# A gated attention and maxout kernel on one core: the order of every engine fixed by hand, one copy per ff2, prefetches spread

## The chip, the cores and the metric

One core of one Trainium2 chip. The metric is the device time in microseconds (us). "Span" is the time from the first to the last instruction in a profile; the device time was 1.7 to 2.1 us longer. The profile names the engines PE (TensorE matmuls), PEld (TensorE weight loads), DVE (VectorE), ACT (ScalarE), POOL (GpSimd) and SP (SyncE).

## The reference

```python
# u, v: (8, 3072, 256)   z: (8, 3072, 64)   w1, w2: (256, 1024)   w_out: (1024, 256), all float32
def _attn_ref(u, v, z):
    scores = (1.0 / S) * np.matmul(z, z.transpose(0, 2, 1))
    attn = np.maximum(scores, 0.0) ** 2
    return u * np.matmul(attn, v)

def _moe_ref(x, w1, w2, w_out):
    return np.maximum(x @ w1, x @ w2) @ w_out

# reference: _moe_ref(_attn_ref(u, v, z).reshape(24576, 256), w1, w2, w_out)
```

The scores are symmetric. So the kernel computes only the blocks on and above the diagonal, and gets the mirrored ones by a transposing DMA. It also uses max(h1, h2) = relu(h1 - h2) + h2. So the first product is x (w1 - w2), called *ff1*; the second, *ff2*, is relu(ff1) w_out plus x (w2 w_out), with both weight differences and products folded once.

## The kernel before

The work comes in 48 groups: 8 batches of 6, each of 512 rows (four tiles of 128). A group has these matmuls:

- score pairs: two matmuls of 64 x 128 weights and 512 columns, one in each half of the array's rows; 42 pairs a batch in all
- attention: 24 units of two matmuls of 512 columns
- ff1 of the group before: 16 matmuls of 512 columns
- ff2 of the group before: 40 matmuls of 256 columns

In PSUM, where the matmuls write, the kernel keeps one accumulator of 2 x 512 fp32 columns and three buffers of the same size (tag `mm`). The three serve everything else in turn: a score pair (`s_ps`), two blocks of ff1 (`d_ps`), all of an ff2 (`o_ps`). To "evict" a buffer is to read it out, after which it is free again. The code, cut:

```python
def ff1(nb, xT, g_sb, on_dve):                  # four times a group, by DVE and ACT in turn
    d_ps = mm_psum.tile([P, 2, GW], fp32, name="d_ps", tag="mm")
    # ... four matmuls ...
    o = g_sb[:, nb : nb + 2, :]
    if on_dve:
        nc.vector.tensor_single_scalar(out=o, in_=d_ps, scalar=0.0, op=ALU.max)
    else:
        nc.scalar.activation(o, d_ps, AF.Relu)

def ff2(b, g, xT, g_sb):
    o_ps = mm_psum.tile([P, G, D], fp32, name="o_ps", tag="mm")
    o_sb = opool.tile([P, G, D], fp32, name="o_sb")
    for t in range(G):
        # ... eight matmuls g_sb x w_out, then two xT x W2o, into o_ps[:, t, :] ...
        if t % 2 == 1:
            nc.scalar.copy(o_sb[:, t - 1 : t + 1, :], o_ps[:, t - 1 : t + 1, :])
    nc.sync.dma_start(...)

with tc.manual_schedule(engines={PE}):          # only TensorE's order is as written
    # ... all scores of group 0 first ...
    for i, (b, g) in enumerate(groups):
        if g == 0 and b + 1 < B:                # all prefetches of a batch at its start
            zTs[b + 1] = zT_dma(load_z(b + 1, 1))
            v_of[b + 1] = load_v(b + 1, 2)
        if b + 1 < B:
            load_u(b + 1, g)
        # ... scores of the next group in up to four bursts, the four ff1 pieces between units:
        order = list(range(g * G, NT)) + list(range(0, g * G))     # mirrored blocks last
        for k, t in enumerate(order):
            for pr in at_w.get(k, ()):
                score_pair(*pr, zTs[nxt[0]])
            if k in at_f:
                ff1(at_f[k], prev[2], g_sb, on_dve=(at_f[k] // 2) % 2 == 0)
            attn_unit(b, g, t, v_of[b], xacc, k == 0, k == NT - 1)
        xT = epilogue(b, g, xacc)               # DVE: xT = xacc * u
        if prev:
            ff2(*prev, g_sb)
```

## Time and profile before

| | before |
|---|---|
| device time | 1108.57 us (1107.86 to 1109.05) |
| third group begins | 111.2 us |
| period of one batch of six groups, steady state | 128.86 us |
| of which matmuls of attention, ff1, ff2 back to back | 6 x 18.18 = 109.1 us |

(The first row is of three runs. With one more the median is 1108.21, which stands in the table of the result.) A batch's period is the distance in the timeline from the end of one ff2 to the end of the sixth after it. "Third group begins" is the first score matmul after the first ff2.

The page of the kernel before: parts 1 and 2, and groups of part 5 (line, engine, operation, tiles, shape, count; busy us and mean ns of one; idle us of the engine before them and who ended most of it).

```profile
span 1106.8 us, 13696 instructions
PE 1004.6 (91%) x5720; PEld 512.5 (46%) x5720; DVE 421.7 (38%) x556; ACT 472.2 (43%) x530; POOL 43.9 (4%) x86
...
PE   6318999999999999999999999999999999999997
...
PEclk8668999999999999999999999999999999999999
...
L203 PE MATMUL o_ps<-w_out_sb,g_sb 128*128 128x256 bf16 x1536 | 199.3, 272 | 32.6 <-ACT o_sb L219 32.3
L185 PE MATMUL d_ps<-xT,w_sb 128*128 128x512 bf16 x768 | 197.0, 380 | 0.0
...
L123 PE MATMUL s_ps<-zT 64*128 64x512 bf16 x672 | 107.9, 390 | 59.0 <-DVE W2o_sb L261 27.8
L219 ACT COPY o_sb<-o_ps 128x512 f32<-128x512 f32 x96 | 56.2, 585 | 245.5 <-PE o_ps L211 242.6
```

TensorE is the busy engine, and two things stand out. The second and third slices (28 to 83 us) are mostly empty, at a granted clock of about 0.6, and the fourth is not yet full, at about 0.8. And ff2 waits for its own copy.

Waits of VectorE (DVE) and TensorE (PE), some of the longest (us in total, times, longest us):

```profile
DVE zd L69 <- DMA zT<-zd: 55.6, 6, 31.8
...
PE o_ps L203 <- ACT o_sb L219: 32.3, 48, 0.7
...
DVE zd L69 <- DMA zn<-in_z_dram: 28.3, 3, 23.3
PE s_ps L123 <- DVE W2o_sb L261: 27.8, 1, 27.8
...
PE s_ps L123 <- ACT r_sb L134: 21.4, 6, 18.6
```

Behind TensorE's two long waits at the start (18.6 and 27.8 us) stand two z copies at the head of VectorE's queue. The first waited for its load, the second for the transpose that still read the same buffer:

```profile
44.96 1.03 DVE L69 COPY zd<-zn 128x1536 bf16<-128x1536 bf16 x2 [23.34 <-DMA zn<-in_z_dram]
83.73 1.03 DVE L69 COPY zd<-zn 128x1536 bf16<-128x1536 bf16 x2 [31.80 <-DMA zT<-zd]
```

Its TensorE timeline (start us, us, engine, line, operation, tiles, count; in brackets the idle time before and its releaser):

```profile
59.40 0.39 PE L123 MATMUL s_ps<-zT 64*128 64x512 bf16 x2
87.55 1.04 PE L123 MATMUL s_ps<-zT 64*128 64x512 bf16 x4 [27.76 <-DVE W2o_sb L261]
...
111.17 1.13 PE L123 MATMUL s_ps<-zT 64*128 64x512 bf16 x6
112.23 1.90 PE L166 MATMUL xacc<-a_sb,v_sb 128*128 128x512 bf16 x8
...
128.88 0.38 PE L211 MATMUL o_ps<-W2o_sb,xT 128*128 128x256 bf16 x2
129.94 1.03 PE L203 MATMUL o_ps<-w_out_sb,g_sb 128*128 128x256 bf16 x8 [0.67 <-ACT o_sb L219]
```

How to read the last two lines. Two matmuls start at 128.88, and 256 columns take 0.109 us each, so the next could start at 129.10. It starts at 129.94: 0.84 us are lost. The bracket says 0.67, because the profile counts idle time only from the modelled end of the matmul before, and a matmul's listed duration is longer than its spacing. In this document "lost" always means the distance from the natural start; it is the larger number.

### The profile page before, as it was taken

The page shows a single profiled execution, that of the slowest core. Times are in us where ns is not written, and L with a number is a line of the kernel's source. Part 1 is how long each engine was busy: PE and PEld are TensorE (multiplying, and loading weights), DVE is VectorE, ACT ScalarE, POOL GpSimd, SP SyncE. Part 2 cuts the span into 40 slices and gives each one's busy share as a digit, 9 for nine tenths or more (in the row PEclk, how much of TensorE's full clock was granted, in tenths as well). Part 3 has the DMA queues.
Part 4 walks back from the last instruction along what each step waited for, and adds up shares of the span by engine and source line. Part 5 has one row for each costly group of instructions (what it writes and reads, how often), then busy time and mean ns, then how long its engine had stood idle before and what let it go on. Part 6 is the DMA issues. An engine that isn't in the chain of part 4 may idle for free.

```text
span 1106.8 us, 13696 instructions
## 1 busy us (share of the span) xinstructions
PE 1004.6 (91%) x5720; PEld 512.5 (46%) x5720; DVE 421.7 (38%) x556; ACT 472.2 (43%) x530; POOL 43.9 (4%) x86
## 2 busy tenths in 40 slices
PE   6318999999999999999999999999999999999997
PEld 2103444445544554454454455445544545544554
DVE  5204334443354333533344332543334332443321
ACT  5213435543365434544255433653345442554322
POOL 3100000000000000000000000000000000000000
PEclk8668999999999999999999999999999999999999
DMA  9999856964699646995579754996559631653300
GB/s 167 134 189 174 144 99 129 167 144 96 100 175 173 110 94 119 147 189 105 94 137 162 145 96 96 124 207 122 92 102 203 122 86 48 115 115 76 77 39 38
DMA packets 341661, 136.94 MB, mean 124 GB/s; under 512 B 324064, under 2 KB 325344, under 8 KB 341600
## 3 DMA queue, kind: packets, MB, share of 16 engines
q1 hardware_dynamic: 328928, 106.19, 49.6%
q0 software_dynamic: 12672, 29.89, 20.2%
q8 instruction: 44, 0.72, 0.3%
q14 instruction: 17, 0.14, 0.0%
HBM read 59.77 MB, written 25.17 MB: 77 GB/s over the span
## 4 chain that ended last, share of the span: by engine, by line
PE 78%; ACT 8%; DMA 5%; issue 3%; DVE 3%; SPq 3%; POOL 0%; ACTq 0%; POOLq 0%; DVEq 0%
PE xacc L166 40%; PE o_ps L203 16%; PE d_ps L185 13%; PE s_ps L123 5%; PE o_ps L211 4%; ACT o_sb L219 4%; ACT r_sb L134 4%; DVE g_sb L194 2%; SPq L141 2%; DMA zn<-in_z_dram 1%; DMA uT<-un 1%; DMA un<-in_u_dram 1%; SPq L88 1%; DMA zT<-zd 1%; DVE a_sb L136 1%
## 5 line engine op out<-in xcount | busy, mean ns | idle before, releaser
L136 DVE TENSOR_TENSOR a_sb<-r_sb 128x1024 bf16<-128x1024 bf16 x336 | 231.1, 692 | 436.9 <-ACT r_sb L134 436.9
L134 ACT ACTIVATE r_sb<-s_ps 128x1024 bf16<-128x1024 f32 x332 | 318.4, 1027 | 164.1 <-PE s_ps L123 144.0
L166 PEld LDWEIGHTS <-v_sb 128*128 128x128 bf16 x2304 | 216.4, 98 | 288.1 <-issue 47.0
L166 PE MATMUL xacc<-a_sb,v_sb 128*128 128x512 bf16 x1344 | 326.9, 384 | 0.0
L166 PE MATMUL xacc<-at_sb,v_sb 128*128 128x512 bf16 x960 | 229.2, 379 | 0.0
L203 PE MATMUL o_ps<-w_out_sb,g_sb 128*128 128x256 bf16 x1536 | 199.3, 272 | 32.6 <-ACT o_sb L219 32.3
L185 PE MATMUL d_ps<-xT,w_sb 128*128 128x512 bf16 x768 | 197.0, 380 | 0.0
L196 ACT ACTIVATE g_sb<-d_ps 128x1024 bf16<-128x1024 f32 x96 | 98.4, 1025 | 214.2 <-PE d_ps L185 155.6
L203 PEld LDWEIGHTS <-g_sb 128*128 128x128 bf16 x1536 | 149.8, 98 | 68.8 <-issue 40.7
L123 PE MATMUL s_ps<-zT 64*128 64x512 bf16 x672 | 107.9, 390 | 59.0 <-DVE W2o_sb L261 27.8
L219 ACT COPY o_sb<-o_ps 128x512 f32<-128x512 f32 x96 | 56.2, 585 | 245.5 <-PE o_ps L211 242.6
L194 DVE TENSOR_SCALAR g_sb<-d_ps 128x1024 bf16<-128x1024 f32 x96 | 117.2, 1221 | 45.2 <-PE d_ps L185 33.4
L185 PEld LDWEIGHTS <-w_sb 128*128 128x128 bf16 x768 | 75.3, 98 | 90.9 <-issue 1.1
L171 DVE SCALAR_TENSOR_TENSOR xT<-xacc,uT 128x512 bf16<-128x512 f32 x96 | 61.8, 686 | 107.3 <-PE xacc L166 107.3
L123 PEld LDWEIGHTS <-zT 64*128 64x128 bf16 x672 | 28.5, 94 | 130.3 <-issue 121.3
L211 PE MATMUL o_ps<-W2o_sb,xT 128*128 128x256 bf16 x384 | 73.3, 273 | 0.0
L86 POOL DMA_DIRECT2D un<-in_u_dram x48 | 25.4, 530 | 651.2 <-DMA uT<-un 649.1
L69 DVE COPY zd<-zn 128x1536 bf16<-128x1536 bf16 (+1 forms) x18 | 8.6, 520 | 83.9 <-DMA zT<-zd 55.6
L211 PEld LDWEIGHTS <-xT 128*128 128x128 bf16 x384 | 37.6, 98 | 4.3
L78 POOL DMA_DIRECT2D v_sb<-in_v_dram x20 | 10.7, 545 | 110.1 <-PE xacc L166 110.1
L103 PE MATMUL tpz<-ident,zd 128*128 128x128 bf16 x24 | 3.1, 308 | 5.7 <-DVE zd L69 5.5
L67 POOL DMA_DIRECT2D zn<-in_z_dram x9 | 4.9, 547 | 42.6 <-DVE zd L69 41.8
(21 smaller groups left out, 24.2 us busy)
## 6 DMA issues: line engine op xcount, KB each, us to landing
out_dram<-o_sb SPq DMA_DIRECT2D x48, 512.0 KB, 4.9
un<-in_u_dram POOLq DMA_DIRECT2D x48, 256.0 KB, 4.9
v_sb<-in_v_dram POOLq DMA_DIRECT2D x14, 768.0 KB, 16.0
zn<-in_z_dram POOLq DMA_DIRECT2D x7, 384.0 KB, 4.6
at_sb<-a_sb SPq DMA_TRANSPOSE x120, 4.6
v_sb<-in_v_dram POOLq DMA_DIRECT2D x6, 256.0 KB, 7.9
uT<-un SPq DMA_TRANSPOSE x48, 3.1
w_121<-in_moe_w_dram POOLq DMA_DIRECT2D x1, 512.0 KB, 12.4
```

What stands on the lines that cost most here:

```text
L86: nc.gpsimd.dma_start(out=un, in_=src[:, ds(g * G, G), :])
L123: nc.tensor.matmul(s_ps[:, h, :], zT[rows, 2 * m + h, :], zT[rows, ds(g * G, G), :].rearrange("p t c -> p (t c)"), start=True, stop=True,)
L134: nc.scalar.activation(r, s_ps, AF.Relu)
L136: nc.vector.tensor_mul(a[:, k : k + 2, :], r, r)
L166: nc.tensor.matmul(o, v_sb[:, t, ts(dc, P)], mv, start=first, stop=last)
L171: nc.vector.scalar_tensor_tensor(out=xT[:, dc, :].rearrange("p (t r) -> p t r", r=P), in0=xacc[:, dc, :].rearrange("p (t r) -> p t r", r=P ...
L185: nc.tensor.matmul(d_ps[:, j, :], w15_sb[:, kc, ts(nb + j, P)], xT[:, kc, :], start=(kc == 0), stop=(kc == KD - 1),)
L194: nc.vector.tensor_single_scalar(out=o, in_=d_ps, scalar=0.0, op=ALU.max)
L196: nc.scalar.activation(o, d_ps, AF.Relu)
L203: nc.tensor.matmul(o_ps[:, t, :], g_sb[:, nb, ts(t, P)], w_out_sb[:, nb, :], start=(nb == 0), stop=False,)
L211: nc.tensor.matmul(o_ps[:, t, :], xT[:, dc, ts(t, P)], W2o_sb[:, dc, :], start=False, stop=(dc == KD - 1),)
L219: nc.scalar.copy(o_sb[:, t - 1 : t + 1, :], o_ps[:, t - 1 : t + 1, :])
```

## The change: its intent and the diff

The intent: let no engine's order be the scheduler's. Every queue is issued in the written order. Mirrored blocks come first in a group, because they were finished longest ago. Scores run ahead across group borders, in bursts of three pairs at units 0, 8 and 16. Each ff2 is copied out once. The next batch's z, u and v are loaded in portions over the groups. The diff, cut (the two lines with "takes all 1024 columns" sum up the code that was there; left out are the sizes of some buffer pools, the copy of W2o, which moved from VectorE to ScalarE, the first group's relus, a third of which VectorE did and which are all ScalarE's now, and the last ff2, written out in halves):

```diff
-    with tc.manual_schedule(engines={PE}):
+    with tc.manual_schedule():
...
 def ff1
-        if on_dve:  ... DVE takes all 1024 columns of this d_ps ...
-        else:       ... ACT takes all 1024 columns ...
+            nc.scalar.activation(g_sb[:, nb, :], d_ps[:, 0, :], AF.Relu)
+            nc.vector.tensor_single_scalar(
+                out=g_sb[:, nb + 1, :], in_=d_ps[:, 1, :], scalar=0.0, op=ALU.max
+            )
...
 def ff2
-            if t % 2 == 1:
-                nc.scalar.copy(o_sb[:, t - 1 : t + 1, :], o_ps[:, t - 1 : t + 1, :])
+            nc.scalar.copy(o_sb, o_ps)
...
+        double_z(0, 0, 4)
+        zT_pe(0, 0, 4, "dve")
+        double_z(0, 4, 8)
+        zT_pe(0, 4, 8, "act")
+        ahead(1)
+        double_z(0, 12, 8)
+        zT_pe(0, 12, 8, "dve")
+        ahead(2)
+        double_z(0, 20, 4)
+        zT_pe(0, 20, 4, "dve")
...
-            order = list(range(g * G, NT)) + list(range(0, g * G))
-            for k, t in enumerate(order):
+            for n in range(NT):
+                k = need[i, n]
+                if done < 12:
+                    ahead(max(k, done + 1))
+                elif k > done or (n in (0, 8, 16) and done + 3 <= k + AHEAD):
+                    ahead(done + 3)
+                attn_unit(b, g, n, acc, n == 0, n == NT - 1)
+                if n == 1 and i + 2 < len(groups):
+                    load_u(*groups[i + 2])
+                if i == 0 and n == 13:
+                    turn_u(0, 0)
+                if n == 20 and i + 1 < len(groups):
+                    turn_u(*groups[i + 1])
+                if b + 1 < B:
+                    if g == 1 and n == 4:
+                        load_z(b + 1, 0, NT)
+                    if g == 2 and n == 4:
+                        double_z(b + 1, 0, NT)
+                        zT_dma(b + 1)
+                    if g >= 1 and n == 8:
+                        load_v(b + 1, (g - 1) * G, G)
...
+            if prev:
+                g_sb = ff(prev)          # all four ff1 pieces, here
             xT = epilogue(b, g, acc)
             if prev:
                 ff2(*prev, g_sb)
```

One thing is easily missed in this diff: ff1 is no longer spread between attention units, but stands as one block directly before ff2. The built program shows another: VectorE's half of a `d_ps` waits for ScalarE's half, although the two read different halves of it.

More of the change, by code (lines that the diff above doesn't have):

```diff
@@ L27 @@
     ALU = mybir.AluOpType
-    PE = mybir.EngineType.PE
     B, S, D = u.shape
@@ L34 @@
     P = 128
+    R = 64
     NT = S // P
@@ L40 @@
     KF = Dff // P
+    AHEAD = 10
     c2 = float((1.0 / S) * (1.0 / S))
@@ L47 @@
     vpool = ctx.enter_context(tc.tile_pool(name="vpool", bufs=2))
-    unat = ctx.enter_context(tc.tile_pool(name="unat", bufs=4))
-    upool = ctx.enter_context(tc.tile_pool(name="upool", bufs=8))
-    apool = ctx.enter_context(tc.tile_pool(name="apool", bufs=8))
-    tpool = ctx.enter_context(tc.tile_pool(name="tpool", bufs=12))
-    rpool = ctx.enter_context(tc.tile_pool(name="rpool", bufs=4))
+    unat = ctx.enter_context(tc.tile_pool(name="unat", bufs=3))
+    upool = ctx.enter_context(tc.tile_pool(name="upool", bufs=4))
+    apool = ctx.enter_context(tc.tile_pool(name="apool", bufs=9))
+    tpool = ctx.enter_context(tc.tile_pool(name="tpool", bufs=13))
+    rpool = ctx.enter_context(tc.tile_pool(name="rpool", bufs=3))
     xpool = ctx.enter_context(tc.tile_pool(name="xpool", bufs=2))
@@ L57 @@
     acc_psum = ctx.enter_context(tc.tile_pool(name="acc_psum", bufs=1, space=bass.MemoryType.PSUM))
-    def load_z(b, chunks):
-        zn = znat.tile([P, NT, dqk], bf16, name="zn")
-        zd = znat.tile([P, NT, 2, dqk], bf16, name="zd")
-        src = z[b].rearrange("(p t) d -> p t d", t=NT)
-        n = NT // chunks
-        for c in range(chunks):
-            sl = ds(c * n, n)
-            nc.gpsimd.dma_start(out=zn[:, sl, :], in_=src[:, sl, :])
-            for h in range(2):
-                nc.vector.tensor_copy(zd[:, sl, h, :], zn[:, sl, :])
-        return zd
@@ L72, in load_v, with by_tile, load_z @@
-    def load_v(b, chunks):
-        v_sb = vpool.tile([P, NT, D], bf16, name="v_sb")
-        src = v[b].rearrange("(p t) d -> p t d", t=NT)
-        n = NT // chunks
-        for c in range(chunks):
-            sl = ds(c * n, n)
-            nc.gpsimd.dma_start(out=v_sb[:, sl, :], in_=src[:, sl, :])
-        return v_sb
-    uT = {}
+    def by_tile(x):
+        return x.rearrange("(p t) d -> p t d", t=NT)
+    zn, zd, zT, v_sb, un, uT = {}, {}, {}, {}, {}, {}
+    def load_z(b, lo, n):
+        if b not in zn:
+            zn[b] = znat.tile([P, NT, dqk], bf16, name="zn")
+            zd[b] = znat.tile([P, NT, 2, dqk], bf16, name="zd")
+            zT[b] = zpool.tile([P, NT, P], bf16, name="zT")
+        sl = ds(lo, n)
+        nc.gpsimd.dma_start(out=zn[b][:, sl, :], in_=by_tile(z[b])[:, sl, :])
@@ new lines, in double_z, with zT_dma, zT_pe @@
+    def double_z(b, lo, n):
+        sl = ds(lo, n)
+        for h in range(2):
+            nc.vector.tensor_copy(zd[b][:, sl, h, :], zn[b][:, sl, :])
+    def zT_dma(b):
+        nc.sync.dma_start_transpose(zT[b], zd[b].rearrange("p t h d -> p (t h d)"))
+    def zT_pe(b, lo, n, engine):
+        tp = mm_psum.tile([P, n, P], bf16, name="tpz", tag="mm")
+        for j in range(n):
+            nc.tensor.transpose(
+                tp[:, j, :], zd[b][:, lo + j, :, :].rearrange("p h d -> p (h d)"), ident
+            )
+        if engine == "act":
+            nc.scalar.copy(zT[b][:, lo : lo + n, :], tp)
+        else:
+            nc.vector.tensor_copy(zT[b][:, lo : lo + n, :], tp)
@@ L83, in load_u, with load_v @@
+    def load_v(b, lo, n):
+        if b not in v_sb:
+            v_sb[b] = vpool.tile([P, NT, D], bf16, name="v_sb")
+        sl = ds(lo, n)
+        nc.gpsimd.dma_start(out=v_sb[b][:, sl, :], in_=by_tile(v[b])[:, sl, :])
     def load_u(b, g):
-        un = unat.tile([P, G, D], bf16, name="un")
-        src = u[b].rearrange("(p t) d -> p t d", t=NT)
-        nc.gpsimd.dma_start(out=un, in_=src[:, ds(g * G, G), :])
+        un[b, g] = unat.tile([P, G, D], bf16, name="un")
+        nc.gpsimd.dma_start(out=un[b, g], in_=by_tile(u[b])[:, ds(g * G, G), :])
@@ L87, in load_u, with turn_u @@
+    def turn_u(b, g):
         t = upool.tile([P, G, KD, P], bf16, name="uT")
         nc.sync.dma_start_transpose(
-            t.rearrange("p a c r -> p (a c) r"), un.rearrange("p a d -> p (a d)")
+            t.rearrange("p a c r -> p (a c) r"), un[b, g].rearrange("p a d -> p (a d)")
         )
         uT[b, g] = t
-    def zT_dma(zd):
-        t = zpool.tile([P, NT, P], bf16, name="zT")
-        nc.sync.dma_start_transpose(t, zd.rearrange("p t h d -> p (t h d)"))
-        return t
-    def zT_pe(zd):
-        t = zpool.tile([P, NT, P], bf16, name="zT")
-        for c in range(0, NT, 4):
-            tp = mm_psum.tile([P, 4, P], bf16, name="tpz", tag="mm")
-            for j in range(4):
-                nc.tensor.transpose(
-                    tp[:, j, :], zd[:, c + j, :, :].rearrange("p h d -> p (h d)"), ident
-                )
-            if (c // 4) % 2 == 0:
-                nc.scalar.copy(t[:, c : c + 4, :], tp)
-            else:
-                nc.vector.tensor_copy(t[:, c : c + 4, :], tp)
-        return t
@@ L113, with score_pair @@
     A = {}
-    def score_pair(b, g, m, zT, on_dve=False):
+    def score_pair(b, g, m):
         blk = m // 2
-        if (b, g, blk) not in A:
+        if m % 2 == 0:
             A[b, g, blk] = apool.tile([P, G, GW], bf16, name="a_sb")
@@ L121, in score_pair @@
         for h in range(2):
-            rows = ds(h * dqk, dqk)
+            rows = ds(h * R, R)
             nc.tensor.matmul(
                 s_ps[:, h, :],
-                zT[rows, 2 * m + h, :],
-                zT[rows, ds(g * G, G), :].rearrange("p t c -> p (t c)"),
+                zT[b][rows, 2 * m + h, :],
+                zT[b][rows, ds(g * G, G), :].rearrange("p t c -> p (t c)"),
                 start=True,
@@ L130, in score_pair @@
         r = rpool.tile([P, 2, GW], bf16, name="r_sb")
-        if on_dve:
-            nc.vector.tensor_single_scalar(out=r, in_=s_ps, scalar=0.0, op=ALU.max)
-        else:
-            nc.scalar.activation(r, s_ps, AF.Relu)
+        nc.scalar.activation(r, s_ps, AF.Relu)
         k = 2 * (m % 2)
@@ L144, in score_pair, with attn_unit @@
             A[b, blk, g] = t
-    def windows(b, g, n=3):
-        ms = list(range(2 * g, NT // 2))
-        k = -(-len(ms) // n)
-        base, extra = divmod(len(ms), k)
-        res, at = [], 0
-        for i in range(k):
-            size = base + (1 if i < extra else 0)
-            res.append([(b, g, m) for m in ms[at : at + size]])
-            at += size
-        return res
-    def attn_unit(b, g, t, v_sb, xacc, first, last):
+    def attn_unit(b, g, t, acc, first, last):
         blk, j = divmod(t, G)
@@ L161, in attn_unit, with epilogue @@
             if blk >= g:
-                o, mv = xacc[:, dc, :], a[:, j, :]
+                o, mv = acc[:, dc, :], a[:, j, :]
             else:
-                o = xacc[:, dc, :].rearrange("p (k r) -> p k r", r=P)
+                o = acc[:, dc, :].rearrange("p (k r) -> p k r", r=P)
                 mv = a[:, :, j, :]
-            nc.tensor.matmul(o, v_sb[:, t, ts(dc, P)], mv, start=first, stop=last)
-    def epilogue(b, g, xacc):
+            nc.tensor.matmul(o, v_sb[b][:, t, ts(dc, P)], mv, start=first, stop=last)
+    def epilogue(b, g, acc):
         xT = xpool.tile([P, KD, GW], bf16, name="xT")
@@ L172, in epilogue @@
                 out=xT[:, dc, :].rearrange("p (t r) -> p t r", r=P),
-                in0=xacc[:, dc, :].rearrange("p (t r) -> p t r", r=P),
+                in0=acc[:, dc, :].rearrange("p (t r) -> p t r", r=P),
                 scalar=c2,
@@ L179, in epilogue @@
         return xT
-    def ff1(nb, xT, g_sb, on_dve):
-        d_ps = mm_psum.tile([P, 2, GW], fp32, name="d_ps", tag="mm")
-        for j in range(2):
-            for kc in range(KD):
-                nc.tensor.matmul(
-                    d_ps[:, j, :],
-                    w15_sb[:, kc, ts(nb + j, P)],
-                    xT[:, kc, :],
-                    start=(kc == 0),
-                    stop=(kc == KD - 1),
-                )
-        o = g_sb[:, nb : nb + 2, :]
-        if on_dve:
-            nc.vector.tensor_single_scalar(out=o, in_=d_ps, scalar=0.0, op=ALU.max)
-        else:
-            nc.scalar.activation(o, d_ps, AF.Relu)
@@ L198, in ff2 @@
-    def ff2(b, g, xT, g_sb):
-        o_ps = mm_psum.tile([P, G, D], fp32, name="o_ps", tag="mm")
-        o_sb = opool.tile([P, G, D], fp32, name="o_sb")
-        for t in range(G):
-            for nb in range(KF):
-                nc.tensor.matmul(
-                    o_ps[:, t, :],
-                    g_sb[:, nb, ts(t, P)],
-                    w_out_sb[:, nb, :],
-                    start=(nb == 0),
-                    stop=False,
-                )
-            for dc in range(KD):
-                nc.tensor.matmul(
-                    o_ps[:, t, :],
-                    xT[:, dc, ts(t, P)],
-                    W2o_sb[:, dc, :],
-                    start=False,
-                    stop=(dc == KD - 1),
-                )
-            if t % 2 == 1:
-                nc.scalar.copy(o_sb[:, t - 1 : t + 1, :], o_ps[:, t - 1 : t + 1, :])
-        nc.sync.dma_start(
-            out=out[ds(b * S, S), :].rearrange("(p t) d -> p t d", t=NT)[:, ds(g * G, G), :],
-            in_=o_sb,
-        )
@@ L226, with ff1 @@
-    zd0 = load_z(0, 2)
-    ident = consts.tile([P, P], bf16)
-    make_identity(nc, ident)
-    v_cur = load_v(0, 6)
-    load_u(0, 0)
-    w1_sb = tpool.tile([P, KD, Dff], bf16, name="w1", tag="at_sb")
-    nc.gpsimd.dma_start(out=w1_sb, in_=moe_w1.rearrange("(c p) f -> p c f", p=P))
-    w2_sb = tpool.tile([P, KD, Dff], bf16, name="w2", tag="at_sb")
-    nc.gpsimd.dma_start(out=w2_sb, in_=moe_w2.rearrange("(c p) f -> p c f", p=P))
+    def ff1(xT, g_sb):
+        for nb in range(0, KF, 2):
+            d_ps = mm_psum.tile([P, 2, GW], fp32, name="d_ps", tag="mm")
+            for j in range(2):
+                for kc in range(KD):
+                    nc.tensor.matmul(
+                        d_ps[:, j, :],
+                        w15_sb[:, kc, ts(nb + j, P)],
+                        xT[:, kc, :],
+                        start=(kc == 0),
+                        stop=(kc == KD - 1),
+                    )
+            nc.scalar.activation(g_sb[:, nb, :], d_ps[:, 0, :], AF.Relu)
+            nc.vector.tensor_single_scalar(
+                out=g_sb[:, nb + 1, :], in_=d_ps[:, 1, :], scalar=0.0, op=ALU.max
+            )
@@ new lines, in ff2 @@
+    def ff2(b, g, xT, g_sb, split=False):
+        dst = by_tile(out[ds(b * S, S), :])[:, ds(g * G, G), :]
+        for t0 in range(0, G, 2 if split else G):
+            n = 2 if split else G
+            o_ps = mm_psum.tile([P, n, D], fp32, name="o_ps", tag="mm")
+            o_sb = opool.tile([P, n, D], fp32, name="o_sb")
+            for t in range(n):
+                for nb in range(KF):
+                    nc.tensor.matmul(
+                        o_ps[:, t, :],
+                        g_sb[:, nb, ts(t0 + t, P)],
+                        w_out_sb[:, nb, :],
+                        start=(nb == 0),
+                        stop=False,
+                    )
+                for dc in range(KD):
+                    nc.tensor.matmul(
+                        o_ps[:, t, :],
+                        xT[:, dc, ts(t0 + t, P)],
+                        W2o_sb[:, dc, :],
+                        start=False,
+                        stop=(dc == KD - 1),
+                    )
+            nc.scalar.copy(o_sb, o_ps)
+            nc.sync.dma_start(out=dst[:, ds(t0, n), :], in_=o_sb)
@@ L235 @@
+    ident = consts.tile([P, P], bf16)
     w_out_sb = consts.tile([P, KF, D], bf16)
-    nc.gpsimd.dma_start(out=w_out_sb, in_=moe_w_out.rearrange("(c p) d -> p c d", p=P))
-    for g in range(1, NG):
-        load_u(0, g)
     w15_sb = consts.tile([P, KD, Dff], bf16)
     W2o_sb = consts.tile([P, KD, D], bf16)
-    def fold_weights():
-        nc.vector.tensor_sub(w15_sb, w1_sb, w2_sb)
-        w2T_sb = tpool.tile([P, KD, KF, P], bf16, name="w2T", tag="at_sb")
-        for dc in range(KD):
-            tp = mm_psum.tile([P, KF, P], bf16, name="tpw", tag="mm")
-            for j in range(KF):
-                nc.tensor.transpose(tp[:, j, :], w2_sb[:, dc, ts(j, P)], ident)
-            nc.scalar.copy(w2T_sb[:, dc, :, :], tp)
-        for dc in range(KD):
-            ps = mm_psum.tile([P, D], fp32, name="w2o_ps", tag="mm")
-            for nb in range(KF):
-                nc.tensor.matmul(
-                    ps,
-                    w2T_sb[:, dc, nb, :],
-                    w_out_sb[:, nb, :],
-                    start=(nb == 0),
-                    stop=(nb == KF - 1),
-                )
-            nc.vector.tensor_copy(W2o_sb[:, dc, :], ps)
@@ L263 @@
-    groups = [(b, g) for b in range(B) for g in range(NG)]
-    FF1_AT = {4: (4, 10, 16, 22), 3: (4, 11, 13, 20), 2: (4, 8, 16, 20), 1: (4, 9, 14, 19), 0: (2, 8, 14, 20)}
-    with tc.manual_schedule(engines={PE}):
-        zTs = {0: zT_pe(zd0)}
-        n = 0
-        for w in windows(0, 0):
-            for pr in w:
-                score_pair(*pr, zTs[0], on_dve=(n % 3 == 1))
-                n += 1
-        v_of = {0: v_cur}
+    groups = [(b, g) for b in range(B) for g in range(NG)]
+    pairs, need = [], {}
@@ new lines, with ahead, ff @@
+    for i, (b, g) in enumerate(groups):
+        for n in range(NT):
+            if n // G >= g and n % 2 == 0:
+                pairs.append((b, g, n // 2))
+            need[i, n] = len(pairs)
+    done = 0
+    def ahead(upto):
+        nonlocal done
+        while done < min(upto, len(pairs)):
+            score_pair(*pairs[done])
+            done += 1
+    def ff(prev):
+        g_sb = gpool.tile([P, KF, GW], bf16, name="g_sb")
+        ff1(prev[2], g_sb)
+        return g_sb
+    with tc.manual_schedule():
+        load_z(0, 0, 4)
+        load_z(0, 4, 8)
+        load_z(0, 12, 12)
+        make_identity(nc, ident)
+        for g in range(NG):
+            load_v(0, g * G, G)
+        load_u(0, 0)
+        w2_sb = tpool.tile([P, KD, Dff], bf16, name="w2", tag="at_sb")
+        nc.gpsimd.dma_start(out=w2_sb, in_=moe_w2.rearrange("(c p) f -> p c f", p=P))
+        load_u(0, 1)
+        w1_sb = tpool.tile([P, KD, Dff], bf16, name="w1", tag="at_sb")
+        nc.gpsimd.dma_start(out=w1_sb, in_=moe_w1.rearrange("(c p) f -> p c f", p=P))
+        nc.gpsimd.dma_start(out=w_out_sb, in_=moe_w_out.rearrange("(c p) d -> p c d", p=P))
+        double_z(0, 0, 4)
[8 more added lines that the diff above has]
+        zT_pe(0, 20, 4, "dve")
@@ L274 @@
         prev = None
         for i, (b, g) in enumerate(groups):
-            if g == 0 and b + 1 < B:
-                zTs[b + 1] = zT_dma(load_z(b + 1, 1))
-                v_of[b + 1] = load_v(b + 1, 2)
-            if b + 1 < B:
-                load_u(b + 1, g)
-            nxt = groups[i + 1] if i + 1 < len(groups) else None
-            ws = windows(*nxt) if nxt else []
-            at_w = {(24 * k) // len(ws): w for k, w in enumerate(ws)}
-            at_f = dict(zip(FF1_AT[len(ws)], range(0, KF, 2))) if prev else {}
@@ L285 @@
-            g_sb = gpool.tile([P, KF, GW], bf16, name="g_sb") if prev else None
-            xacc = acc_psum.tile([P, KD, GW], fp32, name="xacc")
-            order = list(range(g * G, NT)) + list(range(0, g * G))
-            for k, t in enumerate(order):
-                for pr in at_w.get(k, ()):
-                    score_pair(*pr, zTs[nxt[0]])
-                if k in at_f:
-                    ff1(at_f[k], prev[2], g_sb, on_dve=(at_f[k] // 2) % 2 == 0)
-                attn_unit(b, g, t, v_of[b], xacc, k == 0, k == NT - 1)
@@ L294 @@
-            xT = epilogue(b, g, xacc)
+            acc = acc_psum.tile([P, KD, GW], fp32, name="acc")
+            for n in range(NT):
+                k = need[i, n]
[8 more added lines that the diff above has]
+                    turn_u(0, 0)
+                if i == 1 and n == 9:
+                    nc.vector.tensor_sub(w15_sb, w1_sb, w2_sb)
+                if n == 20 and i + 1 < len(groups):
[8 more added lines that the diff above has]
+                        load_v(b + 1, (g - 1) * G, G)
+                    if g == NG - 1 and n == 14:
+                        load_v(b + 1, g * G, G)
@@ new lines @@
+            if i == 0:
+                w2T_sb = tpool.tile([P, KD, KF, P], bf16, name="w2T", tag="at_sb")
+                for dc in range(KD):
+                    tp = mm_psum.tile([P, KF, P], bf16, name="tpw", tag="mm")
+                    for j in range(KF):
+                        nc.tensor.transpose(tp[:, j, :], w2_sb[:, dc, ts(j, P)], ident)
+                    nc.scalar.copy(w2T_sb[:, dc, :, :], tp)
+            elif i == 1:
+                for dc in range(KD):
+                    ps = mm_psum.tile([P, D], fp32, name="w2o_ps", tag="mm")
+                    for nb in range(KF):
+                        nc.tensor.matmul(
+                            ps,
+                            w2T_sb[:, dc, nb, :],
+                            w_out_sb[:, nb, :],
+                            start=(nb == 0),
+                            stop=(nb == KF - 1),
+                        )
+                    nc.scalar.copy(W2o_sb[:, dc, :], ps)
@@ L295 @@
+            if prev:
+                g_sb = ff(prev)
+            xT = epilogue(b, g, acc)
             if prev:
                 ff2(*prev, g_sb)
-            else:
-                fold_weights()
             prev = (b, g, xT)
-        g_sb = gpool.tile([P, KF, GW], bf16, name="g_sb")
-        for nb in range(0, KF, 2):
-            ff1(nb, prev[2], g_sb, on_dve=(nb // 2) % 2 == 0)
-        ff2(*prev, g_sb)
+        g_sb = ff(prev)
+        ff2(*prev, g_sb, split=True)
 _INS = ['u', 'v', 'z', 'moe_w1', 'moe_w2', 'moe_w_out']
```

## The prediction

> **What bounds it now.** TensorE: 1004.6 of 1106.8 us busy (page, part 1). In the steady state its matmuls stand back to back: the timeline shows a 512-column matmul every 0.216 us and a 256-column one every 0.109. The Trainium skill, "TensorE: Matmul & The Clock Gate" (Back-to-back issue gap), gives N/2.4 + 2.5 ns, that is 215.8; the trace agrees. So per group 48 attention + 16 ff1 + 40 ff2 matmuls cost 18.18 us that no order removes. The measured period of a batch of six groups is 128.86 us. Over 6 x 18.18 = 109.1 that holds 42 score pairs x 0.217 = 9.1; 16 bursts of pairs x 0.2 of switching (the skill's "TensorEngine Tiling (Array Packing)", Key Properties, says a change of tiling mode drains the array; the trace shows about 0.2 us per burst); 6 x 0.84 in the middle of ff2 waiting for the half copy (waits: o_ps for o_sb 32.3 us, 48 times); 4 x 0.3 where the third pair of a burst after ff2 waits for the second half copy.
>
> **The start is the loose part.** The third group begins only at 111.2 us. TensorE idles 18.6 us (29 to 48) and 27.8 us (60 to 88) because VectorE's queue stands behind the next batches' z copies, themselves behind loads and transposes; after each the clock restarts low (windows: 0.67, 0.71, 0.55, 0.68).
>
> **What the change does.**
> 1. Start: z in small chunks, one pair per attention unit, prefetches of z, u, v spread over later groups and placed in VectorE's order where data has long landed. My estimate: attention begins near 10 us; ten units at about 1.1 us (ScalarE pitch 0.92 per pair, some cold clock); rest of group 0 until 28; folding 3; group 1 13; second folding 2; ff1 and ff2 9. Third group starts near 54 instead of 111: **-57 us**.
> 2. One copy per ff2: removes 0.84 per group, **-38**.
> 3. ff1 moves from between attention units to directly before ff2. In the built order each d_ps pair is evicted by ScalarE first, and VectorE waits for ScalarE (same tile). So the last eighth of g_sb is ready 0.38 + 0.04 + 0.585 + 0.035 + 0.69 + 0.05 = 1.78 us after the last ff1 matmul begins; ff2 wants it after 0.98. **+0.80 per group, +37.**
> 4. A burst of three now stands at the head of every group but the last two; its third pair needs o_ps's buffer, now freed by one 1024-wide copy (1.02 instead of 0.585): stall 0.74 in six groups of six instead of 0.3 in four: **+3.2 per batch, +24.**
> 5. Bursts 16 to 14 a batch, and fewer odd waits (about 1.3 a batch unexplained above): **-12.** Tail: last output in halves, **-1**.
>
> Steady state: 109.1 + 4.8 + 9.1 + 2.8 + 4.4 = 130.2 per batch against 128.9; slightly worse. The gain is the start.
>
> **Sum.** 54 + 994 (46 groups) + 12.5 tail + 1.8 (time over span, as before) = about 1062 us. Range 1044 to 1085. Faster by over 2%: 0.87; same 0.11; slower 0.02.
>
> **What would show it.** Third group starting at 48 to 60 us; TensorE idle before o_ps for g_sb's VectorE half about 0.8 x 47, none for o_sb inside ff2; s_ps waiting for o_sb about 0.7 x 44; batch period 130. Wrong if: the serial evictions cost less or overlap (period nearer 122, total near 1000-1020); or loads and transposes still starve the start (group 1 waiting for mirrored blocks, weights or v), or the transpose queue falls behind now that mirrored blocks come first in a group (waits of attention matmuls for DMA).

## The result, and the profile after

| | before | after |
|---|---|---|
| device time, median | 1108.21 us | 1078.53 us (1078.11 to 1079.48) |
| span of the profiled run | 1106.8 us | 1076.7 us |
| third group begins | 111.2 us | 68.2 us |
| from there to the end | 995.6 us | 1008.5 us |
| batch period | 128.86 us | 130.49 us |

The ratio is 0.9737 (95% interval 0.9720 to 0.9754). A ratio is the mean time of one kernel's runs over that of the other's of the same rounds, so not quite the ratio of the medians in the table. Executions over 1.5% slower than the fastest of the same kernel are left out of the means.

The start gives 43 us, and the rest takes 13 of them back. The changed kernel is faster although its steady state is slower.

The page of the changed kernel:

```profile
span 1076.7 us, 13801 instructions
PE 1002.7 (93%) x5647; PEld 508.3 (47%) x5720; DVE 433.5 (40%) x650; ACT 483.7 (45%) x583; POOL 59.5 (6%) x115
...
PE   6699999999999999999999999999999999999998
...
PEclk9799999999999999999999999999999999999999
...
L190 PE MATMUL o_ps<-w_out_sb,g_sb 128*128 128x256 bf16 x1536 | 217.1, 274 | 21.6 <-DVE g_sb L178 21.3
...
L205 ACT COPY o_sb<-o_ps 128x1024 f32<-128x1024 f32 (+1 forms) x49 | 48.7, 995 | 220.0 <-PE o_ps L198 220.0
L121 PE MATMUL s_ps<-zT 64*128 64x512 bf16 x672 | 102.6, 384 | 25.6 <-ACT o_sb L205 24.7
```

TensorE's waits in the changed kernel:

```profile
PE s_ps L121 <- ACT o_sb L205: 24.7, 44, 0.6
PE o_ps L190 <- DVE g_sb L178: 21.3, 48, 0.4
PE tpz L85 <- DVE zd L77: 10.0, 4, 4.2
PE acc L150 <- DVE xT L155: 8.5, 1, 8.5
```

The wait for `o_sb` inside ff2 is gone. Two others stand in its place, once in nearly every group: the third score pair behind ff2, and the end of the first ff2 output. Its TensorE timeline:

```profile
42.72 3.57 PE L150 MATMUL acc<-at_sb,v_sb 128*128 128x512 bf16 x8 [8.46 <-DVE xT L155]
46.08 3.19 PE L150 MATMUL acc<-a_sb,v_sb 128*128 128x512 bf16 x8
...
62.93 1.14 PE L190 MATMUL o_ps<-w_out_sb,g_sb 128*128 128x256 bf16 x7
64.51 0.28 PE L190 MATMUL o_ps<-w_out_sb,g_sb 128*128 128x256 bf16 x1 [0.44 <-DVE g_sb L178]
...
68.22 0.60 PE L121 MATMUL s_ps<-zT 64*128 64x512 bf16 x4
69.39 0.39 PE L121 MATMUL s_ps<-zT 64*128 64x512 bf16 x2 [0.56 <-ACT o_sb L205]
```

The eighth matmul of ff2 would start at 62.93 + 7 x 0.109 = 63.69. It starts at 64.51, so 0.82 us are lost. The third score pair would start at 68.22 + 0.44 = 68.66 (0.44 is the distance of a first from a third pair in an undisturbed burst). It starts at 69.39, so 0.73 us are lost. In the kernel before this pair lost 0.3 us, and in four groups of six only. There, three other third pairs of a batch lost time as well, 0.29, 0.29 and 0.44 us: their buffer was a `d_ps` that VectorE was still evicting (1.22 us for 1024 columns). The longest is listed by the profile, here in the first batch:

```profile
186.61 0.39 PE L123 MATMUL s_ps<-zT 64*128 64x512 bf16 x2 [0.28 <-DVE g_sb L194]
```

Per batch the account closes to 0.3 us (us):

| | before | after |
|---|---|---|
| attention, ff1, ff2 matmuls | 109.1 | 109.1 |
| 42 score pairs x 0.217 | 9.1 | 9.1 |
| switching, 0.2 a burst | 16 bursts: 3.2 | 14 bursts: 2.8 |
| inside ff2, waiting for the half copy | 6 x 0.84 = 5.0 | 0 |
| ff2 waiting for the last of g_sb | 0 | 6 x 0.82 = 4.9 |
| third pair waiting for o_ps's buffer | 4 x 0.3 = 1.2 | 6 x 0.73 = 4.4 |
| third pair waiting for VectorE to evict d_ps | 1.0 | 0 |
| sum | 128.6 | 130.3 |
| measured | 128.86 | 130.49 |

### The profile page after: what moved, and what is told of

Same layout as the page of the kernel before. It is cut to its first block, busy times and chain, and to the rows that moved or that the text cites. A ratio compares the mean times of both kernels' runs of the same rounds, so it can differ in the third digit from the quotient of the medians.

```text
span 1076.7 us, 13801 instructions
## 1 busy us (share of the span) xinstructions
PE 1002.7 (93%) x5647; PEld 508.3 (47%) x5720; DVE 433.5 (40%) x650; ACT 483.7 (45%) x583; POOL 59.5 (6%) x115
## 4 chain that ended last, share of the span: by engine, by line
PE 86%; ACT 7%; DVE 4%; issue 1%; SPq 1%; DMA 1%; ACTq 0%; DVEq 0%; POOLq 0%
PE acc L150 47%; PE d_ps L170 15%; PE o_ps L190 13%; PE s_ps L121 6%; ACT o_sb L205 4%; PE o_ps L198 4%; DVE g_sb L178 3%; ACT g_sb L177 3%; SPq L135 1%; ACT r_sb L129 0%; DMA uT<-un 0%; PE tpz L85 0%; DMA zn<-in_z_dram 0%; DVE a_sb L131 0%; PE w2o_ps L299 0%
## 5 line engine op out<-in xcount | busy, mean ns | idle before, releaser
L150 PE MATMUL acc<-a_sb,v_sb 128*128 128x512 bf16 x1281 | 300.1, 382 | 4.3 <-issue 1.4
L190 PE MATMUL o_ps<-w_out_sb,g_sb 128*128 128x256 bf16 x1536 | 217.1, 274 | 21.6 <-DVE g_sb L178 21.3
L178 DVE TENSOR_SCALAR g_sb<-d_ps 128x512 bf16<-128x512 f32 x192 | 132.9, 692 | 243.9 <-ACT g_sb L177 243.8
L150 PE MATMUL acc<-at_sb,v_sb 128*128 128x512 bf16 x960 | 217.2, 382 | 8.5 <-DVE xT L155 8.5
L177 ACT ACTIVATE g_sb<-d_ps 128x512 bf16<-128x512 f32 x192 | 114.6, 597 | 245.7 <-PE d_ps L170 245.7
L170 PE MATMUL d_ps<-xT,w_sb 128*128 128x512 bf16 x758 | 173.1, 379 | 0.5
L205 ACT COPY o_sb<-o_ps 128x1024 f32<-128x1024 f32 (+1 forms) x49 | 48.7, 995 | 220.0 <-PE o_ps L198 220.0
L155 DVE SCALAR_TENSOR_TENSOR xT<-acc,uT 128x512 bf16<-128x512 f32 x96 | 61.4, 681 | 10.3 <-DMA uT<-un 10.3
L97 POOL DMA_DIRECT2D v_sb<-in_v_dram x48 | 25.9, 544 | 0.0
L77 DVE COPY zd<-zn 128x1536 bf16<-128x1536 bf16 (+2 forms) x22 | 8.9, 450 | 3.8 <-DMA zn<-in_z_dram 3.8
```

Of the source, the lines that this page charges most:

```text
L97: nc.gpsimd.dma_start(out=v_sb[b][:, sl, :], in_=by_tile(v[b])[:, sl, :])
L150: nc.tensor.matmul(o, v_sb[b][:, t, ts(dc, P)], mv, start=first, stop=last)
L155: nc.vector.scalar_tensor_tensor(out=xT[:, dc, :].rearrange("p (t r) -> p t r", r=P), in0=acc[:, dc, :].rearrange("p (t r) -> p t r", r=P) ...
L170: nc.tensor.matmul(d_ps[:, j, :], w15_sb[:, kc, ts(nb + j, P)], xT[:, kc, :], start=(kc == 0), stop=(kc == KD - 1),)
L177: nc.scalar.activation(g_sb[:, nb, :], d_ps[:, 0, :], AF.Relu)
L178: nc.vector.tensor_single_scalar(out=g_sb[:, nb + 1, :], in_=d_ps[:, 1, :], scalar=0.0, op=ALU.max)
```

## The experiments

Every kernel below gave a correct result. Each was timed beside runs of the kernel before on the same chip. Those runs scatter between chips and between executions (the medians of their fast runs were 1108.0 to 1111.0 us). The changed kernel itself was not timed again beside the experiments, so a difference of a few us to its 1078.53 says little by itself. Within one trace the full batches in the middle repeat within 0.03 us.

Theory A: the steady state is a chain of small lateness races on TensorE, each worth its own distance, and the start is a question of what stands in front of what in a queue. The rivals differ by experiment and are named in the expectations.

### One copy per ff2, alone, in the kernel before

```diff
-            if t % 2 == 1:
-                nc.scalar.copy(o_sb[:, t - 1 : t + 1, :], o_ps[:, t - 1 : t + 1, :])
+        nc.scalar.copy(o_sb, o_ps)
```

> The kernel before with nothing changed but one 1024-wide copy per ff2 in place of two. Theory A (local latency races decide the steady state): the 0.84 us wait inside ff2 goes in every group (-5.0 us a batch), the third score pair behind ff2 waits 0.74 instead of 0.3 in four groups of six (+1.8), so the batch goes from 128.9 to about 125.6 us and the time from 1108 to about 1083. Rival B (the steady state is held by something else, such as the transposes' and copies' queues, and waits only move): batch within 0.5 us of 128.9, time over 1100.

Measured: 1075.78 us (1070.66 to 1081.11), ratio 0.970 (0.962 to 0.977); batch period 125.57 us. The period is as theory A has it, and rival B falls. The time is 7 us under the expected 1083. Its own runs are 10 us apart, with mean granted clocks of 0.973 to 0.982. In the profiled one (1081.11 us) the third group begins at 110.1 us, about as before, and the rest takes 969.3 instead of 995.6 us: the gain is in the steady state. Why other runs were 10 us faster was not looked into. This one line is worth as much as the whole change, which kept it and gave its gain away elsewhere.

### The first burst of scores two units later

```diff
-                elif k > done or (n in (0, 8, 16) and done + 3 <= k + AHEAD):
+                elif k > done or (n in (2, 8, 16) and done + 3 <= k + AHEAD):
```

> The changed kernel with the first burst of three score pairs at unit 2 instead of unit 0. Theory A: the 44 waits of s_ps for o_sb (0.73 us each over the natural spacing) go, batch 130.5 to about 126.1, time 1078.5 to about 1046. Rival B: the same time appears as a wait elsewhere (r_sb or the d_ps buffers), batch stays within 1 us of 130.5.

Measured: 1046.37 us, ratio 0.943 (0.938 to 0.948); batch period 126.05 us. Rival B falls. TensorE's waits are now:

```profile
PE o_ps L190 <- DVE g_sb L178: 21.2, 48, 0.4
PE acc L150 <- DVE xT L155: 11.6, 1, 11.6
```

The wait of `s_ps` for `o_sb` is gone from the list. Nothing grew in the steady state: the 0.86 us of two attention units cover the copy. (The wait for xT, once at the start, grew from 8.5 to 11.6 us; it is taken up below.)

### A PSUM tile of its own for each 512 columns of ff1

```diff
-            d_ps = mm_psum.tile([P, 2, GW], fp32, name="d_ps", tag="mm")
             for j in range(2):
+                d_ps = mm_psum.tile([P, GW], fp32, name="d_ps", tag="mm")
...
+                if j == 0:
+                    nc.vector.tensor_single_scalar(
+                        out=g_sb[:, nb, :], in_=d_ps, scalar=0.0, op=ALU.max
+                    )
+                else:
+                    nc.scalar.activation(g_sb[:, nb + 1, :], d_ps, AF.Relu)
```

> The changed kernel with each ff1 output of 512 columns in a PSUM tile of its own, VectorE and ScalarE in turn, ScalarE last; so VectorE no longer waits for ScalarE. Theory A: the wait before the last g_sb piece falls from 0.82 to about 0.1 us; three buffers for eight tiles cost back about 0.08 three times; net -0.5 us a group, batch about 127.5, time about 1054. Rival C (the wait is plain eviction time, not the order of ScalarE before VectorE): no change in the wait, batch 130.5 or more.

Measured: 1050.87 us, ratio 0.947 (0.941 to 0.954); batch period 127.08 us. The wait of `o_ps` for `g_sb` is no longer in the list. The engines, operations and shapes of the evictions are the same; only the order between the two engines has been lifted (and which of them comes last; their times differ by 0.09 us, against 0.82 lost). So rival C falls: the lost time was the row ScalarE 0.60, then VectorE 0.69 us, not eviction as such. In the changed kernel the last pair reads:

```profile
85.46 0.60 ACT L177 ACTIVATE g_sb<-d_ps 128x512 bf16<-128x512 f32 x1 [0.27 <-PE d_ps L170]
86.09 0.69 DVE L178 TENSOR_SCALAR g_sb<-d_ps 128x512 bf16<-128x512 f32 x1 [0.17 <-ACT g_sb L177]
```

and with own tiles, in the same place of another group, VectorE is released by TensorE and ScalarE comes last:

```profile
83.73 0.69 DVE L178 TENSOR_SCALAR g_sb<-d_ps 128x512 bf16<-128x512 f32 x1 [0.17 <-PE d_ps L170]
84.04 1.13 PE L192 MATMUL o_ps<-w_out_sb,g_sb 128*128 128x256 bf16 x8
84.24 0.60 ACT L182 ACTIVATE g_sb<-d_ps 128x512 bf16<-128x512 f32 x1 [0.34 <-PE d_ps L170]
```

### The xT terms of ff2 first

(The diff is cut and its lines joined.)

```diff
+                for dc in range(KD):
+                    nc.tensor.matmul(
+                        o_ps[:, t, :], xT[:, dc, ts(t0 + t, P)], W2o_sb[:, dc, :],
+                        start=(dc == 0), stop=False,
+                    )
                 for nb in range(KF):
...
-                for dc in range(KD):
```

> The changed kernel with the two xT x W2o matmuls of each ff2 output first, before the eight of g_sb. Theory A (ff2 stalls by a fixed lateness of the last g_sb piece): two matmuls of 0.109 fit into the wait, 0.82 to 0.60, batch 130.5 to 129.2, time 1078.5 to about 1068. If the wait were not a fixed lateness, no change.

Measured: 1066.56 us, ratio 0.962 (0.957 to 0.967); batch period 129.20 us. That is 0.215 us a group, the two matmuls of 0.109 that now fit into the wait. The lateness is fixed, and whatever is put in front of it counts in full.

### The four ff1 pieces between attention units again

```diff
+                if prev and n in at_f:            # 5, 12, 19, 21
+                    ff1(prev[2], g_sb, (at_f[n],))
                 attn_unit(b, g, n, acc, n == 0, n == NT - 1)
...
-            if prev:
-                g_sb = ff(prev)
```

(The subtraction w1 - w2 moved to unit 1 of the second group, since ff1 needs it earlier.)

> The changed kernel with the four ff1 pieces of the group before placed between attention units again (5, 12, 19, 21), evicted as in the changed kernel, ScalarE then VectorE. Theory A: g_sb is ready when ff2 begins, the 0.82 us wait goes in all groups, nothing else changes; batch 130.5 to about 125.6, time about 1041. Rival C (the two engines' eviction rate bounds it): the wait shows as d_ps or s_ps waiting for buffers, batch over 128.

Measured: 1038.92 us, ratio 0.937 (0.933 to 0.941); batch period 125.56 us. The eviction is still ScalarE, then VectorE, and it costs nothing there. So the 4.9 us a batch come from the two together: the serial eviction and its place directly before its consumer. Either remedy removes most of it.

### The first u block transposed first

```diff
-                if i == 0 and n == 13:
-                    turn_u(0, 0)
+        turn_u(0, 0)                              # before the loop over groups
```

> The changed kernel with the transpose of the first u block issued before the transposes of attention blocks instead of behind five of them. Theory A: the 8.5 us wait of the second group's attention for xT goes (u has landed at 16 us, its transpose lands near 28), and the restart at a low clock with it (16 matmuls take 6.8 instead of 3.6 us); third group near 57 instead of 68 us, time about 1067. Rival D (the transposes are held by the loads' bandwidth whatever their order, and the mirrored block then comes late by as much): third group stays within 3 us of 68.

Measured: 1067.01 us, ratio 0.963 (0.959 to 0.966); the third group begins at 57.6 instead of 68.2 us, and the batch period is unchanged (130.49). Rival D falls. In the changed kernel the u block had landed at 16.2 us, but SyncE's queue held its transpose behind five of attention blocks until 37.5 us (SPq is that queue):

```profile
18.18 19.30 SPq L135 DMA_TRANSPOSE at_sb<-a_sb  x5
```

The first two of the five were slow: issued while the weights were loading, they landed 11.8 and 12.7 us after their issue, the other three after 4.5 to 5.2 (the median over the whole run is 4.5). Rival D has a point there: in `u_first` u's own transpose, now issued while the weights load, took 10.2 us instead of 3.8. But it was issued at 15.9 us and landed at 26.1, before it was needed, and so did the first mirrored block, at 31.4. In this run:

```profile
34.67 0.39 PE L121 MATMUL s_ps<-zT 64*128 64x512 bf16 x2 [0.52 <-ACT w2T L293]
35.00 1.90 PE L150 MATMUL acc<-at_sb,v_sb 128*128 128x512 bf16 x8
36.73 1.89 PE L150 MATMUL acc<-a_sb,v_sb 128*128 128x512 bf16 x8
```

The 16 matmuls start without a wait and take 3.6 us. In the changed kernel they took 6.5 us after the wait (42.72 to 49.20), at a granted clock of 0.78 in the stretch from 40 to 60 us; here it was 1.00.

### All copies of the first z before the first squares

```diff
         double_z(0, 4, 8)
+        double_z(0, 12, 12)
         zT_pe(0, 4, 8, "act")
         ahead(1)
-        double_z(0, 12, 8)
         zT_pe(0, 12, 8, "dve")
         ahead(2)
-        double_z(0, 20, 4)
```

> The changed kernel with all copies of the first z placed before the first squares in VectorE's order. The two waits of the z transposes on TensorE (2.6 and 2.1 us) go, attention begins near 11.5 instead of 14.8 us. Theory A: that is off the chain, which runs through the transposes of attention blocks and then u; the third group moves by less than 1.5 us and the wait for xT grows by what the start gains; time within 2 us of 1078.5. Rival E (the start of attention is on the chain): time about 1074.

Measured: 1077.73 us, 0.8 us under the changed kernel, ratio to the kernel before 0.972 (0.968 to 0.975). The 0.8 us are of different rounds and not to be read; the positions in the trace are. Attention begins at 10.55 instead of 14.79 us, and TensorE then stands at:

```profile
42.38 3.21 PE L150 MATMUL acc<-at_sb,v_sb 128*128 128x512 bf16 x8 [12.05 <-DVE xT L155]
```

The start gained 4.2 us, and the wait for xT grew by 3.6. Rival E falls: the gain was swallowed by the chain through u. The expectation was slightly off: the third group moved by 2.0 us (66.3), not less than 1.5. Most of that is the 16 matmuls after the wait: they took 4.9 us here (42.38 to 47.24), against 6.5.

### The next batch's z early, as the kernel before had it

To `u_first`, so that the wait for xT cannot hide it: z of batch 1 is loaded at unit 1 of the first group, and its copy stands at unit 8 in VectorE's order. (Its later load and copy are dropped; that part of the diff is cut.)

```diff
+                if i == 0 and n == 1:
+                    load_z(1, 0, NT)
+                if i == 0 and n == 8:
+                    double_z(1, 0, NT)
```

> As u_first, with the next batch's z loaded in the first group (as the kernel before did, behind the weights) and its copy put into VectorE's order at unit 8 of the first group. Theory A: VectorE stands at that copy until z has landed near 32 us, and the squares of five pairs stand behind it; TensorE waits about 6 to 9 us for a_sb in the first group; time 6 to 10 us over u_first. Rival F (VectorE has room, or z lands early enough): within 2 us of u_first.

Measured: 1075.09 us, 8.1 us over `u_first`; the third group begins at 64.7 instead of 57.6 us. TensorE waits in the first group for the squares (`a_sb`) that stand behind the copy:

```profile
28.13 2.76 PE L150 MATMUL acc<-a_sb,v_sb 128*128 128x512 bf16 x12
36.54 1.86 PE L150 MATMUL acc<-a_sb,v_sb 128*128 128x512 bf16 x4 [5.65 <-DVE a_sb L131]
```

This is the mechanism behind the 18.6 us in the kernel before, made again on purpose with one load. The 27.8 us came from the same queue, but there the copy waited for a transpose, which this run does not repeat. Rival F falls.

### All repairs together, in two ways

`between_all` is the changed kernel with ff1 between units, the burst at unit 2, the first u first and the z copies first. `own_tiles_all` keeps ff1 before ff2 but has own tiles and xT first; the rest is the same.

> The changed kernel with the four repairs that do not overlap: ff1 between attention units (5, 12, 19, 21), first burst at unit 2, first u transposed first, z copies first. Theory A: both waits per group go, batch 109.1 + 9.1 + 2.8 = 121.0 to 121.6 us; the start gains 11.5 (u_first) and, now that the chain through u is gone, 3 us of the z copies; sum 1038.9 - 33 - 11.5 - 3 = about 991 us. Rival: ff1 pieces and the burst at unit 2 now meet in the three PSUM buffers (d_ps or s_ps waiting), batch over 123, time over 1003.

> The changed kernel with ff1 left in front of ff2, but own tiles, xT first, burst at unit 2, u first, z copies first. Theory A: the waits for g_sb end; own tiles keep about 0.3 us a group of waits for buffers; batch about 122.5, time about 1001, some 8 to 11 us over between_all.

Measured: `between_all` 1001.38 us, ratio 0.907 (0.901 to 0.913), batch period 121.98 us. `own_tiles_all` 1002.86 us, ratio 0.908 (0.901 to 0.916), batch period 122.07 us. The second came as expected. The first missed by 10 us, and its trace gives two reasons. The repaired start runs into the next queue: attention of the second group waits 3.2 us for the first mirrored block's transpose, so the z copies' 3 us did not come. And one group of six took 21.62 us instead of 20.76:

```profile
60.47 0.61 PE L121 MATMUL s_ps<-zT 64*128 64x512 bf16 x4
61.76 0.39 PE L121 MATMUL s_ps<-zT 64*128 64x512 bf16 x2 [0.69 <-DVE g_sb L178]
```

That group is the one in which VectorE copies the next batch's z, at unit 4, just before it has to evict the ff1 piece of unit 5. So the rival was right in kind, ff1 pieces and a burst meeting in the three PSUM buffers, though at the burst of unit 8 and in one group of six.

### The z copy of later batches at unit 13

```diff
-                    if g == 2 and n == 4:
+                    if g == 2 and n == 13:
                         double_z(b + 1, 0, NT)
                         zT_dma(b + 1)
```

> As between_all, with the copy of the next batch's z at unit 13 of group 2 instead of unit 4. In between_all one group of six takes 21.62 instead of 20.76 us: there the third pair of the burst at unit 8 waits 0.69 us for VectorE's half of d_ps, which stands behind two z copies of 0.5 us. Theory: with the copies after the piece at unit 12 that wait goes, batch 121.98 to about 121.1, time about 995. If the wait had another cause, no change (1001).

Measured: 995.77 us (995.50 to 997.16), ratio 0.899 (0.897 to 0.901), batch period 121.12 us. This is the fastest version, 7.7% under the changed kernel by the medians (995.77 over 1078.53, of different rounds). All the waits of TensorE that its profile lists, in 994 us:

```profile
PE tpz L85 <- DVE zd L77: 5.2, 2, 4.1
PE acc L150 <- DMA at_sb<-a_sb: 3.0, 1, 3.0
PE s_ps L121 <- ACT r_sb L129: 0.6, 1, 0.6
PE o_ps L190 <- DVE g_sb L178: 0.4, 1, 0.4
```

Its batch is the 109.1 + 9.1 + 2.8 = 121.0 of the account above, to within 0.1.

## Why the prediction was right or wrong

The time was forecast at 1062 us, with 1044 to 1085 as the range. It was 1078.53: inside, 16.5 us above the forecast. The forecast "faster by over 2%" at 0.87 held (2.6%).

- **"Steady state: 130.2 per batch against 128.9; slightly worse. The gain is the start."** Right: 130.49. From the third group on the sum gave 994 + 12.5 = 1006.5 us; it was 1008.5.
- **Step 2, one copy, -38 (0.84 per group).** Right. The wait is gone from the trace, and the copy alone in the kernel before gives the expected period (125.57).
- **Step 3, ff1 before ff2 with serial evictions, +0.80 per group.** Right: 0.82. It was argued from the built order and shown by three runs: own tiles, ff1 between units, and xT first, which takes away exactly its 0.22.
- **Step 4, third pair behind ff2, 0.74 in six groups of six.** Right: 0.73. Moving the burst by two units gives it back.
- **Step 5, fewer odd waits, -12, tail -1.** Held in sum, not tested by itself. The prediction counted 1.3 us a batch as gone without knowing what they were, and that was luck. The trace of the kernel before shows 1.0 of them: the three third pairs that wait for VectorE to evict `d_ps`. In the changed kernel, where ff1 no longer stands between the bursts, no third pair waits for a `d_ps`.
- **Step 1, the start, "Third group starts near 54 instead of 111: -57 us".** The direction was right, the size wrong: 68.2 us, so -43. This is the term that was mis-sized, and it makes up 14 of the 16 us. By its own parts: group 0 ended at 31.2 and not at 28 us, the second group's attention then waited 8.5 us for xT, for which the sum had no term, and it took 15.0 instead of 13 us, the first matmuls at a low clock. The rest of the start was as estimated. Two things were missed. The order of VectorE and SyncE had been written by hand, but nobody had asked, for the first group, what stands in front of what. (a) The u block, landed at 16 us, waited until 37.5 us behind five transposes, two of them slow; with the restart at a low clock that cost 10.6 us (`u_first`). (b) Two z copies stood behind squares that waited for ScalarE, so attention began at 14.8 and not 10 us; but that was off the chain (`z_copies_first`), until (a) was repaired. The prediction named the class ("loads and transposes still starve the start"), not the instance.

What the runs do not tell apart: whether "mirrored blocks first in a group" is worth anything by itself. No wait of TensorE for a mirrored block's DMA shows in the steady state of the changed kernel. In the kernel before, where they came last, none shows either. Nor are the 43 us of the start divided among the parts of the change: the small z chunks, the scores one pair a unit, the later prefetches, VectorE's written order, and the copy of W2o that moved to ScalarE (it was VectorE's copy of W2o that TensorE waited 27.8 us for). Only one early z load was put back, and it cost 8.1 us.

## What to carry to other kernels

When one wait on the busiest engine is removed, look at once at who takes the freed buffer next, and when: here a copy twice as wide freed its buffer 0.4 us later (1.01 instead of 0.58), and a score pair that had been 0.3 us late was 0.73 us late. Do not put a producer whose eviction is serial (here two engines that read one tile in turn) directly before the consumer that needs all of it; in `ff1_between` the three attention units between them cost nothing and covered it. And when the order of a queue is fixed by hand, walk through the first group with the landing times in hand: the queue's head, not the data, decided here, and a gap on TensorE was paid again in the slower matmuls after it (6.5 instead of 3.6 us for 16).

## What the Trainium skill lacked or had wrong

- "TensorE: Matmul & The Clock Gate", Back-to-back issue gap: the formula N/2.4 + 2.5 ns held for a stream in which every matmul has its own weight load (16 matmuls of 512 columns from 78.34 to 81.80 us, 0.216 each). The page's remark that such a stream sustains about 131 ns at N = 512, and that the formula over-counts there, was not borne out: apart from the score pairs, which share the array, no two 512-column matmuls in the traces of `before`, the changed kernel and `between_z_later` start less than 0.215 us apart.
- "TensorEngine Tiling (Array Packing)", Key Properties: that a change of tiling mode drains the array is stated without a size. In the fastest version a group with one burst of three pairs takes 19.04 us and one without takes 18.18: 0.86, of which the pairs are 3 x 0.217. So going into the 64-row mode and back costs about 0.2 us.
- "DMA: Bandwidth & Descriptors", DMA Transpose (X-bar): the section gives no latency for a transpose between other transfers. Here a transpose of an attention block took 4.5 us from issue to landing in the median of the changed kernel, and 11.8 and 12.7 us for the two issued while weights were loading; u's transpose stood behind them in SyncE's queue.
- No page that was read gives, for compute instructions, the distance from one engine's end to the start of another that waits for it. Here it was 0.05 us from ScalarE's or VectorE's end to TensorE's start, and about 0.04 us from a matmul's modelled end to ScalarE.
